# A fourth outer product split into seven inner products, in the first layer of two token chunks

## The chip, the cores and the metric

The kernel runs on one core of a Trainium2 chip. The metric is the device time of one execution in microseconds (us). Engines are called PE (TensorE), DVE (VectorE), ACT (ScalarE), POOL (GpSimd) and SP (the queue that issues most DMAs). Each engine takes its instructions strictly in the order in which they were issued.

## The reference

Attention with a hash mask over 4 x 8 heads of 768 tokens and 64 features, then a two-layer network on the 3072 x 512 result:

```python
scores = np.where(q_bucket == k_bucket, scale * q @ k.T, -1e9)
attn = softmax(scores) @ v               # (4, 8, 768, 64) -> x of (3072, 512)
h = x @ w_in                             # w_in  (512, 2048)
r = np.maximum(h, 0.0)
out = (r * r) @ w_out                    # w_out (2048, 512)
```

All of it is fp32.

## The kernel before

Attention comes first and fills the first 315 us. The network then takes the 3072 tokens in three chunks of 1024 (`i` = 0, 1, 2). For each chunk the first layer (`hidden` or `hidden_pair`) makes five sums of gated blocks, `b11, b12, b21, b22, b_t`, and the second layer (`project`) turns them into the output. The change is in the first layer of chunks 1 and 2.

**The outer scheme.** Each matrix product is done as 2 x 2 blocks with seven block products instead of eight (Strassen's scheme in Winograd's form). The first layer's blocks are halves of the features (256), of the hidden units (1024) and of the tokens (512). One row `r` of 128 hidden units (there are 8 in a half, `NR`) therefore has seven *outer products*, each of two matmuls of 128 x 128 by 512 columns. They are numbered by weight factor and go with a combination of x: 0 with "11", 1 with "21", 2 with "t4", 3 with "t1", 4 with "t2", 5 with "t3", 6 with "22". `w_unit` holds the weight factors of one row in the places that `PLACE` names. Chunk 0 does all seven so, in `hidden`.

**The inner scheme.** Chunks 1 and 2 go by *pairs* of rows (`hidden_pair(i, n, half)`, rows `n` and `n + 4`, four pairs in a chunk, half 0 and half 1). Products 1, 2 and 6 of both rows of a pair are done together, once more as 2 x 2 blocks (two rows, two feature blocks, two token quarters of 256): seven *inner products* of one 128 x 128 matmul by 256 columns in place of eight. `inner_steps` returns these seven in four steps, with the engines' work that belongs to them. In PSUM they use `acc1`, into which products 0, 4, 5 and 2 are added one after the other, with a copy on ScalarE taken between them (`one`, `two`, `three`); `acc2`; and `last`, a part of the tile `acc3`, whose two banks are the two sides. A is the set for product 1, C for product 2, B for product 6. `put(unit, out, other)` adds the outer part and gates one row: `gated` is relu(h) * h in a single VectorE operation (L921).

Products 0, 3, 4 and 5 of each row stay outer products (L1108) in `hidden_pair`; 0, 4 and 5 add up in `acc0`, again with a ScalarE copy between them (`keep`, L1116), and 3 goes into `acc2`. Matmuls of the inner sets are on L1061.

**Order.** The order of every engine is written out by hand (`tc.manual_schedule()`): an engine's instructions run as the Python code issues them, and the framework adds only semaphore waits for data and for reused buffers. Buffers named "h" (`new_h`, five of them, `NH`) hold the halves of a row until it is gated; a new one waits until an earlier holder has been read for the last time. `mark` is a Square over part of q or k on ScalarE (`peak`, L891), four in a pair, whose sums decide on a fallback that does not run here. Weights of the next pair come on SP's queue: `load_unit` (one row's `w_unit`, two buffers) and nine loads of `load_inner` and `load_third_inner`.

**The second layer.** `project(i)` runs seven outer products `k`, each as seven inner products of four matmuls of 256 columns (`product`, L844). In each, `hook` issues VectorE work after the second inner product has been issued, and ScalarE copies out (`one`, `two`, `five`, `three`) stand in ScalarE's queue in the order of issue. `sums_inner` makes the x sums that the inner sets read; for A, B and C it ran in the hooks of k = 5 and k = 6 of the layer before. `inner_sums(0, ...)` makes, a pair at a time, those that product k = 0 reads.

## Time and profile before

| | |
|---|---|
| median of 3 runs | 856.15 us (855.42 to 856.63) |
| the profiled execution | 855.04 us, its span 853.2 us |
| attention | up to 315.5 us in the span |
| network, chunk 0 (both layers) | 315.5 to 496.4 us |
| first layer, chunk 1 | 496.4 to 588.0 us |
| second layer, chunk 1 | 588.0 to 672.6 us |
| first layer, chunk 2 | 672.6 to 764.1 us |
| second layer, chunk 2 | from 764.1 us |

Times in profile lines are from the start of the span. In a row of groups, `x600 | 133.0, 379 | 0.0` reads: 600 instructions, 133.0 us busy in all, 379 ns each on average, 0.0 us idle just before them. In timeline rows the columns are start, duration, engine, line, operation, tiles written and read; a bracket at the end gives the engine's idle time before it and whom it waited for.

### The profile page before, as it was taken

To read this page: it belongs to the slowest core of one execution; us is meant where nothing else is said; L and a number is where in the kernel's file an instruction comes from. 1 tells how busy PE (TensorE), PEld (TensorE's weight loads), DVE (VectorE), ACT (ScalarE), POOL (GpSimd) and SP (SyncE) were. 2 spreads that over 40 slices of the span, in tenths; PEclk is the share of its full clock that TensorE was granted. 3 is DMA by queue.
4 is the path that set the end of the run, shared out by engine and by line. 5 is a ranking of instruction groups with operands and counts; after the bars stand their busy time and mean duration, and the time that the engine had idled before them with its cause. 6 is when DMAs were issued, how large, how long until landed. Compare 5 with 4: busy or idle time off the path is not lost.

```text
span 853.2 us, 17058 instructions
## 1 busy us (share of the span) xinstructions
PE 847.0 (99%) x6625; PEld 526.5 (62%) x6625; DVE 749.3 (88%) x1025; ACT 402.4 (47%) x752; POOL 167.4 (20%) x282
## 2 busy tenths in 40 slices
PE   8999999999999999999999999999999999999998
PEld 4544444444444444444788866667888765668886
DVE  5999999999999988988899968888988788889777
ACT  6877777888877752222211145554111355541111
POOL 2311111123221101543122121111000311200003
PEclk9999999999999999999999999999999999999999
DMA  9776988979998526999976985437647865335467
GB/s 213 137 152 143 183 181 203 209 158 258 242 227 217 170 69 225 342 313 297 340 250 220 275 214 189 160 111 283 192 155 189 205 219 171 128 118 161 140 172 147
DMA packets 232052, 170.12 MB, mean 199 GB/s; under 512 B 164712, under 2 KB 189104, under 8 KB 231968
## 3 DMA queue, kind: packets, MB, share of 16 engines
q1 hardware_dynamic: 192272, 87.78, 41.3%
q0 software_dynamic: 16512, 42.45, 15.9%
q10 hardware_dynamic: 23184, 38.78, 14.6%
q8 instruction: 53, 0.87, 0.4%
q14 instruction: 31, 0.25, 0.1%
HBM read 127.14 MB, written 41.16 MB: 197 GB/s over the span
## 4 chain that ended last, share of the span: by engine, by line
PE 97%; DVE 1%; DMA 1%; issue 0%; ACT 0%; SPq 0%; ACTq 0%; DVEq 0%
PE acc L844 39%; PE st L438 18%; PE xo L492 15%; PE acc L1108 13%; PE acc L1061 9%; PE tot L541 2%; PE hash L368 1%; DMA out_dram<-h 1%; DMA qk_nat<-in_q_dram 0%; PE tp L324 0%; DVE h L1224 0%; DVE o L1210 0%; DVE tmp L1210 0%; DVE bits L418 0%; DVE sum L1210 0%
## 5 line engine op out<-in xcount | busy, mean ns | idle before, releaser
L444 ACT ACTIVATE e<-st 128x768 f32<-128x768 f32 x192 | 155.4, 810 | 57.8 <-PE st L438 54.7
L438 PE MATMUL st<-feat 64*64 64x384 f32 x1536 | 156.9, 483 | 0.1
L492 PE MATMUL xo<-e,v_nat 64*64 64x385 f32 (+1 forms) x1520 | 156.7, 483 | 0.0
L844 PE MATMUL acc<-b,leaf 128*128 128x256 f32 x600 | 133.0, 379 | 0.0
L844 PEld LDWEIGHTS acc<-b,leaf 128*128 128x128 f32 x600 | 113.9, 190 | 16.0 <-issue 0.5
L480 DVE TENSOR_TENSOR total<-total,e 128x1536 f32<-128x1536 f32 x64 | 111.8, 1746 | 4.3 <-ACT e L444 2.8
L404 POOL DMA_DIRECT2D bits<-signed x120 | 61.9, 520 | 216.8 <-ACT signed L393 199.9
L492 PEld LDWEIGHTS xo<-e,v_nat 64*64 64x64 f32 (+1 forms) x1520 | 55.5, 133 | 68.2 <-issue 60.2
L1108 PE MATMUL acc<-t_x,w_unit 128*128 128x512 f32 x192 | 90.9, 595 | 0.0
L438 PEld LDWEIGHTS st<-feat 64*64 64x64 f32 x1536 | 55.4, 133 | 38.9 <-issue 34.9
L844 PE MATMUL acc<-t,leaf 128*128 128x256 f32 x336 | 76.0, 379 | 0.0
L844 PEld LDWEIGHTS acc<-t,leaf 128*128 128x128 f32 x336 | 63.8, 190 | 8.8 <-issue 0.2
L921 DVE SCALAR_TENSOR_TENSOR b<-h 128x512 f32<-128x512 f32 x96 | 65.7, 691 | 3.0
L438 PE MATMUL st<-bits 64*64 64x384 bf16 x768 | 64.7, 325 | 0.3 <-DVE bits L422 0.2
L844 PE MATMUL acc<-x,w_unit 128*128 128x512 f32 x128 | 56.5, 593 | 0.0
L851 ACT COPY two<-acc 128x256 f32<-128x256 f32 (+1 forms) x29 | 12.5, 431 | 87.5 <-PE acc L844 65.9
L844 PE MATMUL acc<-b_t,leaf 128*128 128x256 f32 x240 | 53.8, 379 | 0.0
L1108 PEld LDWEIGHTS acc<-t_x,w_unit 128*128 128x128 f32 x192 | 35.8, 190 | 26.7 <-issue 23.0
L1229 POOL DMA_DIRECT2D out_dram<-h x24 | 15.5, 655 | 181.9 <-DVE h L1224 181.9
L844 PEld LDWEIGHTS acc<-b_t,leaf 128*128 128x128 f32 x240 | 45.6, 190 | 6.2
L851 ACT COPY one<-acc 128x256 f32<-128x256 f32 (+1 forms) x29 | 12.5, 431 | 78.2 <-PE acc L844 58.8
L438 PEld LDWEIGHTS <-bits 64*64 64x64 bf16 x768 | 23.2, 107 | 38.0 <-issue 37.9
(180 smaller groups left out, 1289.0 us busy)
## 6 DMA issues: line engine op xcount, KB each, us to landing
leaf<-w_out ACTq DMA_DIRECT2D x142, 256.0 KB, 3.1
raw<-in_moe_w_in_dram SPq DMA_DIRECT2D x8, 1024.0 KB, 6.7
raw<-in_moe_w_out_dram SPq DMA_DIRECT2D x8, 1024.0 KB, 7.9
w_unit<-w_in SPq DMA_DIRECT2D x16, 512.0 KB, 4.1
w_unit<-w_in SPq DMA_DIRECT2D x8, 896.0 KB, 9.0
w_out<-sums POOLq DMA_DIRECT2D x16, 448.0 KB, 8.0
v_nat<-in_v_dram SPq DMA_DIRECT2D x16, 384.0 KB, 5.2
x_all<-x_t SPq DMA_DIRECT2D x16, 384.0 KB, 3.3
```

The source lines that it names most:

```text
L404: nc.gpsimd.dma_start(out=t[h * D:h * D + NBITS + 1, w, c * HS:(c + 1) * HS], in_=signed[at:at + NBITS + 1, h],)
L438: nc.tensor.matmul(out=st[k * HK:(k + 1) * HK, h, 0:HS], lhsT=src[1][rows, key], rhs=src[0][rows, cut], start=first, stop=not first, skip_ ...
L444: nc.scalar.activation(out=key_of(pr, kt)[:, :, i, 0:HS], in_=st[:, :, 0:HS], func=ACTF.Exp, scale=scale)
L480: nc.vector.tensor_tensor(out=totals[pr], in0=totals[pr], in1=e, op=ALU.add)
L492: return nc.tensor.matmul(out=outs[pr][h * D:(h + 1) * D, c, 0:HS + 1], lhsT=nat[pr, "v_nat"][rows, h, kt * D:(kt + 1) * D], rhs=key_of(pr ...
L541: done = nc.tensor.matmul(out=spares[pr][g * 32:(g + 1) * 32, c2, 0:QS], lhsT=ones[rows], rhs=totals[pr][rows, h, c, c2 * QS:(c2 + 1) * QS ...
L844: nc.tensor.matmul(out=acc[to], lhsT=a(i), rhs=b(i), start=first and i == 0, stop=last and i == n - 1, skip_group_check=True,)
L851: nc.scalar.copy(out=t, in_=acc[of])
L921: nc.vector.scalar_tensor_tensor(out=out, in0=h, scalar=0.0, in1=h, op0=ALU.max, op1=ALU.mult)
L1061: nc.tensor.matmul(out=out, lhsT=w(a), rhs=b, start=start, stop=stop, skip_group_check=True)
L1108: nc.tensor.matmul(out=to, lhsT=w[:, PLACE[a], f], rhs=bt[b](f), start=first and f == 0, stop=last and f == NFT // 2 - 1, skip_group_check ...
L1229: queue.dma_start(out=out[at, m0 + a * 32:m0 + (a + 1) * 32].rearrange("(c i) j -> i c j", i=32), in_=ot[a * 32:(a + 1) * 32].rearrange("i ...
```

## The change

Product 3 (with "t1") of both rows of a pair becomes a fourth inner set, D (`j` = 3). Its weight sums live in `w_unit` itself: `load_unit` loads one more block for the pair's first row, and `sum_unit` forms four sums of 128 columns on VectorE, one pair ahead (for a chunk's first pair, in the second layer before). Its x sums are made by `sums_inner(i, (3,))` in the first pair, where those of set 1 move too.

The sets now run two at a time: A and D step by step in half 0, C and B in half 1; before, A, B and C were spread with one or two between two outer products. `acc2` is no longer used by outer products. The steps `two` and `five` are copied straight into the "h" buffers (D's first unit takes the buffer `five`), and the additions that follow are put into `adds`.

The gate of b22 moves from VectorE (one operation) to ScalarE (`gate_b22`, Relu and then Square). Three parts at the end of a pair (`behind_pair`: the b21 units and two differences on VectorE, the gate of row n + 4 on ScalarE) are issued inside the next pair's half 0, and for the last pair in the hook of k = 0 of the second layer. The `tmp` tiles of the second layer become two halves of one tile.

```diff
@@ load_unit, and new functions beside it
+            if n >= NR and n % 2 == 0:
+                nc.sync.dma_start(out=w_unit[n][:, 4], in_=w_in_7[NQ + r, :, PLACE[3]])
+    def own_factors(w):
+        a = PLACE[3]
+        return (w[:, a, 0], w[:, a, 1], w[:, 4, 1]) + tuple(w[:, 5 + n // 2, n % 2] for n in range(4))
+    def sum_unit(n):
+        if n < NCHUNK * NR:
+            w = w_unit[n]
+            a11, a12, a22, *sums = own_factors(w)
+            sums_a(a11, a12, w[:, 4, 0], a22, *sums)
@@ inner_steps
+            side = j % 2
+            one = three = t_inner[i][3 * side][3]
+            last = snaps[i][:, side, 0:QN]
+            def new(unit):
+                if j == 3 and unit == 0:
+                    return p_r.tile([P, 512], FP32, name="five", bufs=KEPT["five"])
+                return new_h()
...
             def step_1():
-                hs["a2"] = last
-                mul(hs["a0"], 4, t[:, 1], False, False)
-                nc.scalar.copy(out=two, in_=hs["a0"])
-                mul(hs["a2"], 3, t[:, 0], True, False)
-                nc.scalar.copy(out=five, in_=hs["a2"])
+                mul(hs["a0"], 4, t[1], False, False)
+                nc.scalar.copy(out=hs[0][:, QN:HN], in_=hs["a0"])
+                mul(last, 3, t[0], True, False)
+                hs[1] = new(1)
+                nc.scalar.copy(out=hs[1][:, QN:HN], in_=last)
 
             def step_2():
                 mul(hs["a0"], 5, t3, False, False)
                 nc.scalar.copy(out=three, in_=hs["a0"])
-                mul(hs["a2"], 6, y22, False, True)
-                nc.vector.tensor_tensor(out=hs[0][:, QN:HN], in0=hs["a2"], in1=two, op=ALU.add)
-                hs[1] = new_h()
-                nc.vector.tensor_tensor(out=hs[1][:, QN:HN], in0=three, in1=five, op=ALU.add)
+                mul(last, 6, y22, False, True)
+
+            def adds():
+                for unit, by in (0, last), (1, three):
+                    h = hs[unit][:, QN:HN]
+                    nc.vector.tensor_tensor(out=h, in0=h, in1=by, op=ALU.add)
@@ hidden_pair, as it is after the change
+            def gate_b22(r, h):
+                nc.scalar.activation(out=h, in_=h, func=ACTF.Relu)
+                nc.scalar.activation(out=b22[:, r], in_=h, func=ACTF.Square)
...
+            add(0, "11", True, False)
+            one = keep("one")
             if half == 0:
                 A[0]()
+                D[0]()
+                if n == 0:
+                    sums_inner(i, (1,))
+                else:
+                    behind_pair[0]()
+            else:
+                B[0]()
+                C[0]()
+                gate_b22(r0, fives[0])
+                B[1]()
+                A[4](1, b11[:, r], one)
+                if n + 1 < NQ:
+                    sum_unit(i * NR + 2 * n + 2)
+            mark(0)
+            add(4, "t2", False, False)
+            two = keep("two")
+            if half == 0:
+                A[1]()
+                D[1]()
+                if n:
+                    behind_pair[1]()
             else:
                 B[2]()
+                C[1]()
+                B[3]()
+                C[2]()
+                B[5]()
                 B[4](0, b12[:, r0], now["two"])
+                C[5]()
+                add_in(two, fives[1])
+                B[4](1, b12[:, r], two)
                 minus(b_t[:, r0], b12[:, r0], b11[:, r0])
+                minus(b_t[:, r], b12[:, r], b11[:, r])
+                inner_sums(0, slice(n, n + 1))
+            mark(1)
+            add(5, "t3", False, True)
+            three = keep("three")
             if half == 0:
                 A[2]()
+                D[2]()
+                A[3]()
+                D[3]()
+                A[5]()
+                D[5]()
+                add_in(two, fives[0])
+                add_in(fives[0], three)
                 A[4](0, b11[:, r], one)
+                if n:
+                    behind_pair[2]()
             else:
                 C[3]()
+                three_0 = now["three"]
+                def sums():
+                    minus(b12[:, r0], b22[:, r0], b12[:, r0])
+                    add_in(fives[1], three)
+                    C[4](0, b21[:, r0], three_0)
+                    C[4](1, b21[:, r], three)
+                behind_pair[:] = (
+                    sums, lambda: gate_b22(r, fives[1]),
+                    lambda: minus(b12[:, r], b22[:, r], b12[:, r]),
+                )
@@ project
                     sum_x(i + 1, 2)
+                    sum_unit((i + 1) * NR)
...
                     y21 = b[:, NQ:NR, 0:QN]
                     minus(y21, y21, t2)
+                    if k == 0:
+                        for step in behind_pair:
+                            step()
+                        behind_pair.clear()
...
-                        sums_inner(i + 1, (0, 1))
+                        sums_inner(i + 1, (0,))
```

More of the change, by code (lines that the diff above doesn't have):

```diff
@@ L951, in hidden @@
             )
-        w_inner, t_inner, snaps, now = {}, {}, {}, {}
+        w_inner, t_inner, snaps, now, behind_pair = {}, {}, {}, {}, []
         thirds = {}
@@ L1028, in quarters_x @@
         def quarters_x(i, j):
-            x = xs[i][0]
-            b = (x[:, 2:4, 0:HN], x[:, 0:2, HN:NCH], x[:, 2:4, HN:NCH])[j]
+            x, t_x = xs[i]
+            b = (x[:, 2:4, 0:HN], x[:, 0:2, HN:NCH], x[:, 2:4, HN:NCH], t_x[0])[j]
             return b[:, 0, 0:QN], b[:, 0, QN:HN], b[:, 1, 0:QN], b[:, 1, QN:HN]
@@ L1036, in sums_inner, with inner_steps @@
             for j in js:
-                t = p_y.tile([P, NQ, QN], FP32, name=f"t{j}", **({"bufs": 2} if j < 2 else {}))
+                if j < 3:
+                    tile = p_y.tile([P, NQ, QN], FP32, name=f"t{j}", **({"bufs": 2} if j < 2 else {}))
+                    t = [tile[:, m] for m in range(NQ)]
+                else:
+                    os = [p_y.tile([P, HN], FP32, name="o", bufs=NOUT) for _ in range(2)]
+                    t = [o[:, m * QN:(m + 1) * QN] for o in os for m in range(2)]
                 t_inner.setdefault(i, {})[j] = t
                 y11, y12, y21, y22 = quarters_x(i, j)
-                minus(t[:, 0], y12, y11)
-                minus(t[:, 1], y22, t[:, 0])
-                minus(t[:, 2], y21, t[:, 1])
+                minus(t[0], y12, y11)
+                minus(t[1], y22, t[0])
+                minus(t[2], y21, t[1])
                 minus(y12, y22, y12)
-        def inner_steps(i, n, j):
-            w, t = w_inner[i, n][j], t_inner[i][j]
+        def inner_steps(i, n, j, w):
+            t = t_inner[i][j]
             y11, t3, y21, y22 = quarters_x(i, j)
-            hs = {}
-            if i not in snaps:
-                o = [p_y.tile([P, HN], FP32, name="o", bufs=NOUT) for _ in range(2)]
-                o = [o[m // 2][:, m % 2 * QN:(m % 2 + 1) * QN] for m in range(3)]
-                snaps[i] = o, [t_inner[i][m][:, 3] for m in range(3)], spare("acc3")
-            side = (3 * n + (0, 2, 1)[j]) % 2
-            one, two, five = snaps[i][side]
-            three = one
-            last = snaps[i][2][:, side, 0:QN]
+            if i not in snaps:
+                snaps[i] = spare("acc3")
+            side = j % 2
+            one = three = t_inner[i][3 * side][3]
+            last = snaps[i][:, side, 0:QN]
+            hs = {}
+            def new(unit):
+                if j == 3 and unit == 0:
+                    return p_r.tile([P, 512], FP32, name="five", bufs=KEPT["five"])
+                return new_h()
             def mul(out, a, b, start, stop):
@@ L1069, in step_0 @@
                 mul(a1, 1, y21, True, True)
-                hs[0] = new_h()
+                hs[0] = new(0)
                 nc.vector.tensor_tensor(out=hs[0][:, 0:QN], in0=a1, in1=one, op=ALU.add)
@@ L1083, in step_2 @@
                 nc.scalar.copy(out=three, in_=hs["a0"])
-                mul(hs["a2"], 6, y22, False, True)
-                nc.vector.tensor_tensor(out=hs[0][:, QN:HN], in0=hs["a2"], in1=two, op=ALU.add)
-                hs[1] = new_h()
-                nc.vector.tensor_tensor(out=hs[1][:, QN:HN], in0=three, in1=five, op=ALU.add)
+                mul(last, 6, y22, False, True)
[3 more added lines that the diff above has]
+                    nc.vector.tensor_tensor(out=h, in0=h, in1=by, op=ALU.add)
             def step_3():
-                mul(hs["a0"], 2, t[:, 2], False, True)
+                mul(hs["a0"], 2, t[2], False, True)
                 nc.scalar.copy(out=hs[1][:, 0:QN], in_=hs["a0"])
@@ L1096, in put @@
                 gated(out, h)
-            return step_0, step_1, step_2, step_3, put
+            return step_0, step_1, step_2, step_3, put, adds, hs
         def hidden_pair(i, n, half):
@@ L1104, in hidden_pair, with add @@
             acc = ps_m.tile([P, 512], FP32, name="acc0")
-            def add(to, a, b, first, last):
+            def add(a, b, first, last):
                 for f in range(NFT // 2):
                     nc.tensor.matmul(
-                        out=to, lhsT=w[:, PLACE[a], f], rhs=bt[b](f),
+                        out=acc, lhsT=w[:, PLACE[a], f], rhs=bt[b](f),
                         start=first and f == 0, stop=last and f == NFT // 2 - 1,
@@ L1112, in add, with keep @@
                     )
-            def keep(of, name):
-                t = p_r.tile([P, 512], FP32, name=name, bufs=KEPT[name])
-                nc.scalar.copy(out=t, in_=of)
+            def keep(name):
+                if (name, half) == ("two", 0):
+                    t = p_y.tile([P, HN], FP32, name="tmp")
+                else:
+                    t = p_r.tile([P, 512], FP32, name=name, bufs=KEPT[name])
+                nc.scalar.copy(out=t, in_=acc)
                 return t
@@ L1120, in mark, with add_in @@
                 peak(2 * ((i - 1) * NR + 2 * n + half) + m)
+            def add_in(out, by):
+                nc.vector.tensor_tensor(out=out, in0=out, in1=by, op=ALU.add)
+            def gate_b22(r, h):
+                nc.scalar.activation(out=h, in_=h, func=ACTF.Relu)
+                nc.scalar.activation(out=b22[:, r], in_=h, func=ACTF.Square)
             if half == 0:
@@ L1124, in hidden_pair @@
                 load_third_inner(i, n + 1, nc.sync)
-                now["A"], now["C"], now["B"] = (inner_steps(i, n, j) for j in range(3))
-            A, B, C = (now[c] for c in "ABC")
-            add(acc, 0, "11", True, False)
-            one = keep(acc, "one")
+                if n == 0:
+                    sums_inner(i, (3,))
+                own = own_factors(w)
+                now["A"] = inner_steps(i, n, 0, w_inner[i, n][0])
+                now["D"] = inner_steps(i, n, 3, lambda a: own[a])
+            else:
+                C, B = (inner_steps(i, n, j, w_inner[i, n][j]) for j in (1, 2))
@@ L1129, in hidden_pair @@
+            A, D = now["A"], now["D"]
+            fives = D[6]
+            add(0, "11", True, False)
+            one = keep("one")
             if half == 0:
                 A[0]()
+                D[0]()
+                if n == 0:
+                    sums_inner(i, (1,))
+                else:
+                    behind_pair[0]()
+            else:
+                B[0]()
[5 more added lines that the diff above has]
+                    sum_unit(i * NR + 2 * n + 2)
@@ L1131, in hidden_pair @@
+            mark(0)
[6 more added lines that the diff above has]
+                    behind_pair[1]()
             else:
                 B[2]()
-                C[0]()
-                A[4](1, b11[:, r], one)
+                C[1]()
+                B[3]()
+                C[2]()
+                B[5]()
                 B[4](0, b12[:, r0], now["two"])
-            mark(0)
@@ L1137, in hidden_pair @@
-            other = ps_m.tile([P, 512], FP32, name="acc2")
-            add(other, 3, "t1", True, True)
-            five = keep(other, "five")
-            if half == 0:
-                A[1]()
-            else:
-                B[3]()
-                C[1]()
-                minus(b_t[:, r0], b12[:, r0], b11[:, r0])
-                minus(b12[:, r0], b22[:, r0], b12[:, r0])
-            add(acc, 4, "t2", False, False)
-            two = keep(acc, "two")
+                C[5]()
+                add_in(two, fives[1])
@@ L1149, in hidden_pair @@
+                B[4](1, b12[:, r], two)
+                minus(b_t[:, r0], b12[:, r0], b11[:, r0])
+                minus(b_t[:, r], b12[:, r], b11[:, r])
[3 more added lines that the diff above has]
+            three = keep("three")
             if half == 0:
                 A[2]()
-                B[0]()
-                A[4](0, b11[:, r], one)
-                nc.vector.tensor_tensor(out=two, in0=two, in1=five, op=ALU.add)
-            else:
-                C[2]()
-                nc.vector.tensor_tensor(out=two, in0=two, in1=five, op=ALU.add)
-                B[4](1, b12[:, r], two)
-                minus(b_t[:, r], b12[:, r], b11[:, r])
-                inner_sums(0, slice(n, n + 1))
-                C[4](0, b21[:, r0], now["three"])
@@ L1161, in hidden_pair @@
-            mark(1)
-            add(acc, 5, "t3", False, True)
-            three = keep(acc, "three")
-            if half == 0:
-                A[3]()
-                B[1]()
-                gate_sum(b22[:, r], three, five)
+                D[2]()
[5 more added lines that the diff above has]
+                add_in(fives[0], three)
+                A[4](0, b11[:, r], one)
+                if n:
+                    behind_pair[2]()
@@ L1168, in hidden_pair @@
             else:
                 C[3]()
-                gate_sum(b22[:, r], three, five)
-                minus(b12[:, r], b22[:, r], b12[:, r])
-                C[4](1, b21[:, r], three)
+                three_0 = now["three"]
[8 more added lines that the diff above has]
+                )
@@ L1210, in add_to @@
             nc.vector.tensor_tensor(out=out, in0=one, in1=two, op=ALU.add)
+        turns = []
         def whole(one, two):
@@ L1215, in whole @@
                 return one
-            t = p_y.tile([P, QN], FP32, name="tmp", bufs=2)
-            add_to(t, one, two)
-            return t
+            turns.reverse()
+            add_to(turns[0], one, two)
+            return turns[0]
         def put_out(i, ih, jh, n, o):
@@ L1272, in project @@
             V, W, U, X = (p_y.tile([P, 4, QN], FP32, name=f"sum{n}") for n in range(4))
+            tmp = p_y.tile([P, HN], FP32, name="tmp")
+            turns[:] = tmp[:, 0:QN], tmp[:, QN:HN]
             outs = {}
```

## The prediction

> **What bounds the kernel now.** I read the head of the page first, then the chain of work that ended last, and then the same chain in order of time.

> ```profile
> span 853.2 us, 17058 instructions
> PE 847.0 (99%) x6625; PEld 526.5 (62%) x6625; DVE 749.3 (88%) x1025; ACT 402.4 (47%) x752; POOL 167.4 (20%) x282
> PEclk9999999999999999999999999999999999999999
> PE 97%; DVE 1%; DMA 1%; issue 0%; ACT 0%; SPq 0%; ACTq 0%; DVEq 0%
> ```

> TensorE (PE) is busy 99% of the span at full clock and is 97% of the chain. In the stage that the change edits, the chain in order of time (start, us, engine, line, records; an fp32 product is two records) shows one pair, and then the start of the second layer:

> ```profile
> 519.33 1.72 PE acc L1108 x4
> 521.05 0.86 PE acc L1061 x4
> 521.91 1.72 PE acc L1108 x4
> ...
> 526.21 1.73 PE acc L1061 x8
> ...
> 539.98 1.79 PE acc L1108 x4
> 542.21 1.72 PE acc L1108 x4
> ...
> 587.96 84.61 PE acc L844 x392
> ```

> An outer product (L1108, two 512-column matmuls) takes 1.72 us, one 256-column inner product (L1061) 1.73/4 = 0.432, and a pair 542.21 - 519.33 = 22.88. By count that is 8 x 1.72 + 21 x 0.432 = 22.83, so TensorE stands still for 0.05 us in a pair. Whatever the change saves in products it gets in full, if it adds no wait; every wait that it adds is paid in full.

> How close the others are is seen in the busy times of that pair (columns: window, sum, PE, PEld, DVE, ACT, POOL, each with its instructions, clock, DMA share, GB/s):

> ```profile
> 519.30:542.20 22.90, 22.90 (x76) 14.00 (x75) 18.98 (x35) 12.84 (x32) 4.29 (x9) 1.00 0.51 175
> ```

> VectorE (DVE) is busy 83% and ScalarE (ACT) 56%, so both have room on average. What decides is order: all engines take their instructions in turn.

> **What TensorE gains.** Each pair loses two outer products (the t1 product of each half) and gets seven inner products: 2 x 1.72 - 7 x 0.432 = 0.42 us. If the present 0.05 us of waiting goes too, it is 0.46 us, and over the 8 pairs (4 in each of two chunks) **-3.7 us**. A pair would then take 6 x 1.72 + 28 x 0.432 = 22.42 us.

> The other engines' work in a pair, counted in the code: VectorE has 22 operations of 512 columns and 12 of 256, and will have 20, 15 and 4 of 128; ScalarE has 8 copies of 512, 15 of 256 and 4 peak steps, and will have 6, 20, 4 and two gates of two passes. By the times below ScalarE goes from 11.7 us to 14.5 in 22.4: more, and still not full.

> **The durations for the walk.** The timeline around the end of chunk 2's pairs gives start-to-start times (start, us, engine):

> ```profile
> 584.71 1.03 PE L1061 MATMUL acc<-x,sum 128*128 128x256 f32 x4
> 584.91 0.58 ACT L1116 COPY two<-acc 128x512 f32<-128x512 f32 x1 [1.34 <-PE acc L1108]
> 585.39 0.38 ACT L1083 COPY t<-acc 128x256 f32<-128x256 f32 x1
> 585.57 1.96 PE L1108 MATMUL acc<-t_x,w_unit 128*128 128x512 f32 x4
> 585.66 0.86 ACT L891 ACTIVATE raw_qk<-raw_qk 128x768 f32<-128x768 f32 x1
> 586.12 0.42 DVE L1087 TENSOR_TENSOR h<-t,t 128x256 f32<-128x256 f32 x1
> 586.40 0.20 ACT L891 ACTIVATION_READ_ACCUMULATOR raw_qk<-raw_qk 128x1 f32 x1
> 586.45 0.69 DVE L1156 TENSOR_TENSOR two<-two,five 128x512 f32<-128x512 f32 x1
> 587.17 0.69 DVE L1095 TENSOR_TENSOR h<-h,two 128x512 f32<-128x512 f32 x1
> 587.37 0.59 PE L1061 MATMUL acc<-t,sum 128*128 128x256 f32 x2
> 587.57 0.59 ACT L1116 COPY three<-acc 128x512 f32<-128x512 f32 x1 [0.97 <-PE acc L1108]
> 587.89 0.69 DVE L921 SCALAR_TENSOR_TENSOR b<-h 128x512 f32<-128x512 f32 x1
> 588.62 0.69 DVE L600 TENSOR_TENSOR b_t<-b,b 128x512 f32<-128x512 f32 x1
> 589.23 0.42 DVE L600 TENSOR_TENSOR t<-b 128x256 f32<-128x256 f32 x1
> 589.68 0.42 DVE L600 TENSOR_TENSOR t<-b,t 128x256 f32<-128x256 f32 x1
> 590.02 0.42 DVE L600 TENSOR_TENSOR b<-b 128x256 f32<-128x256 f32 x1
> ...
> 595.07 1.22 DVE L600 TENSOR_TENSOR b<-b,t 128x1024 f32<-128x1024 f32 x1
> 596.20 1.22 DVE L600 TENSOR_TENSOR t<-b 128x1024 f32<-128x1024 f32 x1
> ```

> VectorE: 512 columns 0.72 to the next if that reads its result (586.45 to 587.17), 0.60 if not (588.62 to 589.23); 256 columns 0.45 and 0.34; 1024 columns 1.13. ScalarE: a 512-column copy 0.48, a 256-column copy 0.27, the peak step 0.94 (585.66 to 586.40, and 0.20). Hand-overs: a product's result is copied 0.20 after TensorE goes on (587.37, 587.57). TensorE follows a copy's end by 0.16: `two` ends at 585.49, and the matmul behind it (1.96, not 1.88) got going 0.08 after 585.57. VectorE to ScalarE takes 0.10:

> ```profile
> 523.05 0.68 DVE L930 TENSOR_TENSOR h<-three,five 128x512 f32<-128x512 f32 x1
> ...
> 523.83 0.58 ACT L1116 COPY five<-acc 128x512 f32<-128x512 f32 x1 [1.05 <-DVE h L930]
> ```

> The new Relu and Square of 512 columns in SBUF are not in the trace. The nearest rows are the 0.58 of the copy above, and a 512-column Relu with a bias tile:

> ```profile
> L166 ACT ACTIVATE small<-power,excess 128x512 uint8<-128x512 uint32 x32 | 23.0, 717 | 0.7 <-DVE power L150 0.7
> ```

> I take 0.65 between 0.58 and 0.72: Relu 0.70 until Square, which reads it (0.05 more, as on VectorE), and Square 0.55 to the next, which overlaps it by 0.10, as copies do. [...]

> **Three new waits**, walked from the start of a pair (0) with nothing late: outer product 1 to 1.72, A[0] and D[0] to 3.45, product t2 to 5.17, A[1] 6.03, D[1] 6.89, product t3 8.61, A[2] and D[2] 10.34, then A[3]; the second half starts at 11.20.

> *Wait 1, D[1], every pair.* Step 1's second product writes acc3 (`last`). A and D now run it one right behind the other, on two halves of one tile, and the built program makes D's wait for the ScalarE copy of A's. A's ends at 6.03, its copy runs from 6.23 to 6.61, TensorE goes on at 6.77 and not at 6.46: 0.31, x 8 = **2.5 us**. Before, a 1.72 us outer product lay between such steps.

> *Wait 2, A[3], pairs 2 to 4 of a chunk.* All five "h" buffers are held when a pair ends: D's second unit, B's two and C's two. In the next pair A takes B's, and D's second unit the one of C's first unit, which is free only when `behind_pair[0]` has gated that into b21. So the ScalarE copy in D[1] waits for VectorE, whose queue runs without a gap from B[5] of the pair before; B[5] starts when C[2]'s last product is readable, at 20.25 + 0.20 of that pair, that is -1.97. Then: B[5] and C[5] 4 x 0.34; B[4](0) 0.72 + 0.60; add_in 0.72; B[4](1) 0.72 + 0.60; two b_t 1.20; inner_sums 0.45 + 0.34 + 0.34; A[0], D[0] 0.68; minus and add_in 1.20; C[4](0) 0.72 + 0.73 to its end: 10.4, so 8.4. ScalarE copies at 8.5 (to 8.8), Relu to 9.5, Square to 10.0, the peak step to 11.0, `three` to 11.45; A[2]'s copy ends at 11.85, and A[3], which adds into the bank just copied, goes at 12.0. TensorE was there at 10.34 + 0.31. **1.35 us** x 6 = **8.1 us**. Queued behind that one copy are thus both gate steps, the peak step, `three` and A[2]'s copy; TensorE waits for the last of them.

> *Wait 3, the first product of the second layer.* The rest of the last pair is issued in the hook of k = 0. VectorE, from -1.97 again: 7.05 to the end of inner_sums (5.1); the hook's 1024-column minus 1.13 (6.2); minus 0.60; add_in 0.69 (7.5). ScalarE's Relu starts at 7.6, Square at 8.3, and the copy of `two`, queued behind both, at 8.9; it ends at 9.25, TensorE goes on at 9.4. Four groups of four products, 4 x 1.73, had it there at 6.9: **2.5 us** x 2 = **5.0 us**. Then nothing is late: k = 1 starts at some 14.6, and what it reads first leaves VectorE by 10.8 (C[4] twice 1.32, minus 0.60, after 7.5).

> **Costs taken at nothing.** The added weight load (128 KB, 4 times a chunk, on SP's queue in front of nine loads for the next pair) and sum_unit's four 128-column operations, at most 4 x 0.42, which wait for it:

> ```profile
> w_unit<-w_in SPq DMA_DIRECT2D x16, 512.0 KB, 4.1
> sum<-w_in SPq DMA_DIRECT2D x16, 128.0 KB, 4.1
> ```

> They are issued as D[3] ends, and VectorE comes to them some 5 us later, 4.1 needed. It next waits for C[2], some 3 us after; that is the cover, and beyond it each microsecond of late landing moves wait 2 by one. The eight sums of `sums_inner` moved or added in pair 1 (3.2 us) stand where no `behind_pair` is queued.

> **Sum.** 855.04 us is the profiled execution's time, 1.8 above its span; -3.7 + 2.5 + 8.1 + 5.0 = +11.9 gives 866.9. The median of the runs is 1.1 higher (856.15), so **868.0 us**. Bounds: gate 0.58 to 0.72, twice in 8 stalls, -1.1 to +1.1; wait 1 absent -2.5, and with it a pair's A[3] is reached sooner, which wait 2 gives back; each VectorE walk 0.3 short or 0.5 long, x 8, -2.4 to +4.

> [...] L921 gates 512 columns in one VectorE operation of 0.69 us; ScalarE needs two of about 0.65. [...] With the gate on VectorE, 1.25 us leave ScalarE's queue in waits 2 and 3, so that 0.1 of each wait 2 and nothing of wait 3 would be left: 12.5 us less, 855.5, if VectorE has room for two more gates in a pair.

> **Rivals.**
> *The count alone (faster).* ScalarE is idle 44% of a pair; if the copy in D[1] finds its buffer free before 6.9 (decides: VectorE's backlog at a pair's start under 6.8 us and not 10.4), waits 2 and 3 vanish and so, if acc3's halves are independent, does wait 1: 856.15 - 3.7 = 852.5. For: the room above. Against: the queue of single steps is fixed. 3%.
> *Wait 2 half hidden.* VectorE keeps ahead because TensorE's own waits give it time: two of the six remain, 868.0 - 5.4 = 862.6. Against: B[5] starts anew from TensorE in each pair. 12%.
> *Late weights (slower still).* sum_unit's loads land over 8 us after issue, as with the page's 9.0 for 896 KB; in-order VectorE then starts B[5] 2 us late, 6 x 2 = 12: 880. Decides at 8 us. 8%.
> *The change does nothing* (products saved equal waits added, within the 0.2%, 1.7 us, that runs of this kernel can tell from no change): 856. 2%.

> **Numbers.** The forecast has 75%, with 864 to 872 as its own range. 861.5 to 874.5 takes in the half-hidden case and leaves out count alone, nothing and late weights. Faster 0.03, same 0.02, slower 0.95.

> **What would show it.** In the changed profile: a pair of about 24.1 us in the chain (22.7 for a chunk's first), the second layer's first product 2.5 us longer; waits listed as PE behind ScalarE copies (`last` 0.3 us x 8, `three` 1.3 x 6, `two` of the second layer 2.4 x 2), and ScalarE's copy into h behind VectorE's gate into b21. Pairs of 22.4 us would prove the count alone; ScalarE or VectorE waiting for a load of w_unit, late weights.

## The result and the profile after

The change makes the kernel slower: a median of 869.61 us (six runs, 867.61 to 871.01) against 856.44 us of the kernel before on the same chip (855.42 to 857.02), a ratio of 1.0154 (95% interval 1.0141 to 1.0167). 868.0 us had been forecast, within 861.5 to 874.5. The profiled execution took 867.61 us, 12.57 more than before.

The head of the page after the change, the busy times and the shares of the chain:

```profile
span 866.1 us, 17328 instructions
...
PE 849.2 (98%) x6673; PEld 535.4 (62%) x6673; DVE 753.3 (87%) x1073; ACT 425.1 (49%) x808; POOL 167.4 (19%) x282
...
PE 86%; DVE 9%; ACT 2%; issue 1%; POOL 0%; ACTq 0%; DVEq 0%; POOLq 0%
```

Before, TensorE was 97% of the chain; now VectorE (9%) and ScalarE (2%) hold pieces of it: TensorE waits for them in turn.

To compare kernels apart from the start and the end of the program I use the *network stretch*, from the network's first product to the last matmul. Its two ends in the timeline of before:

```profile
315.43 1.98 PE L844 MATMUL acc<-x,w_unit 128*128 128x512 f32 x4
...
849.32 0.44 PE L1260 MATMUL acc<-ident,o 128*128 128x128 f32 x2 [0.52 <-DVE o L1210]
```

and of after:

```profile
316.41 1.98 PE L858 MATMUL acc<-x,w_unit 128*128 128x512 f32 x4
...
861.05 0.44 PE L1324 MATMUL acc<-ident,o 128*128 128x128 f32 x2 [0.52 <-DVE o L1272]
```

533.89 us became 544.64, +10.75. The other 2.1 us of the longer span lie where the code is the same: 0.98 ahead of 316.41, 1.1 behind the last matmul. These two ends differ by more between profiles of one and the same code there: 315.43 and 3.9 in the kernel before, 317.92 and 5.1 in e7 below.

Two pairs of chunk 1 in the view by windows (the first pair, then the second):

```profile
497.36:520.08 22.72, 22.69 (x81) 15.12 (x81) 14.53 (x35) 14.12 (x35) 4.13 (x8) 1.00 0.67 185
520.08:543.90 23.82, 22.92 (x81) 15.04 (x80) 19.10 (x40) 15.60 (x39) 4.25 (x9) 1.00 0.53 173
```

A pair took 22.88 before. The first of a chunk is shorter now, as forecast (22.7), the others longer (23.82; forecast 24.1). Where the second pair loses time is seen in its timeline (rows of PE and ScalarE):

```profile
526.10 1.32 PE L1082 MATMUL acc<-o,w_unit 128*128 128x256 f32 x4
...
528.56 0.37 ACT L1100 COPY h<-acc 128x256 f32<-128x256 f32 x1 [1.45 <-DVE b L935]
528.83 0.64 ACT L1153 ACTIVATE h<-h 128x512 f32<-128x512 f32 x1
...
529.49 0.63 ACT L1154 ACTIVATE b<-h 128x512 f32<-128x512 f32 x1
...
530.03 0.83 ACT L905 ACTIVATE raw_qk<-raw_qk 128x768 f32<-128x768 f32 x1
...
530.85 0.56 ACT L1142 COPY three<-acc 128x512 f32<-128x512 f32 x1
...
531.32 0.37 ACT L1104 COPY t<-acc 128x256 f32<-128x256 f32 x1
...
531.74 0.70 PE L1082 MATMUL acc<-t,sum 128*128 128x256 f32 x2 [0.87 <-ACT t L1104]
```

The first row is wait 1: four records (two products) that take 1.03 without a wait take 1.32. The others are wait 2 with the whole queue: D[1]'s copy waits 1.45 for VectorE's gate into b21, then Relu, Square, peak step, `three` and A[2]'s copy follow without a gap, and A[3] is the last row. Wait 3, in the second layer's first product:

```profile
599.33 0.69 DVE L1118 TENSOR_TENSOR h<-h,three 128x512 f32<-128x512 f32 x1
599.45 0.63 ACT L1153 ACTIVATE h<-h 128x512 f32<-128x512 f32 x1 [5.26 <-DVE h L1149]
...
600.11 0.63 ACT L1154 ACTIVATE b<-h 128x512 f32<-128x512 f32 x1
...
600.65 0.35 ACT L865 COPY two<-acc 128x256 f32<-128x256 f32 x1
...
601.05 1.13 PE L858 MATMUL acc<-b,leaf 128*128 128x256 f32 x4 [1.83 <-ACT two L865]
```

ScalarE stood idle for 5.26 us in front of the Relu, because that comes first in its queue, ahead of the copy of `two` that TensorE waits for.

### The profile page after: what moved, and what is told of

It reads as the page before. It is cut to its first block, busy times and chain, and to the rows that moved or that the text cites. A ratio compares the mean times of both kernels' runs of the same rounds, so it can differ in the third digit from the quotient of the medians.

```text
span 866.1 us, 17328 instructions
## 1 busy us (share of the span) xinstructions
PE 849.2 (98%) x6673; PEld 535.4 (62%) x6673; DVE 753.3 (87%) x1073; ACT 425.1 (49%) x808; POOL 167.4 (19%) x282
## 3 DMA queue, kind: packets, MB, share of 16 engines
q10 hardware_dynamic: 23184, 38.78, 14.5%
## 4 chain that ended last, share of the span: by engine, by line
PE 86%; DVE 9%; ACT 2%; issue 1%; POOL 0%; ACTq 0%; DVEq 0%; POOLq 0%
PE acc L858 39%; PE st L438 18%; PE xo L492 14%; PE acc L1082 7%; PE acc L1131 4%; DVE h L1118 2%; DVE b L935 2%; PE tot L541 2%; DVE h L1110 1%; PE hash L368 1%; DVE b L600 1%; DVE b_t L600 1%; ACT raw_qk L905 1%; DVE two L1149 1%; DVE h L1149 1%
## 5 line engine op out<-in xcount | busy, mean ns | idle before, releaser
L1131 PE MATMUL acc<-t_x,w_unit 128*128 128x512 f32 x128 | 60.1, 592 | 0.0
L935 DVE SCALAR_TENSOR_TENSOR b<-h 128x512 f32<-128x512 f32 x80 | 54.6, 691 | 2.5
L865 ACT COPY two<-acc 128x256 f32<-128x256 f32 (+1 forms) x29 | 12.5, 430 | 81.5 <-PE acc L858 69.1
L865 ACT COPY one<-acc 128x256 f32<-128x256 f32 (+1 forms) x29 | 12.5, 431 | 78.2 <-PE acc L858 63.6
L1110 DVE TENSOR_TENSOR h<-h,acc 128x256 f32<-128x256 f32 x24 | 10.1, 419 | 41.6 <-PE acc L1082 34.5
## 6 DMA issues: line engine op xcount, KB each, us to landing
w_unit<-w_in SPq DMA_DIRECT2D x16, 512.0 KB, 4.1
```

The costliest lines, as they stand in the source:

```text
L865: nc.scalar.copy(out=t, in_=acc[of])
L935: nc.vector.scalar_tensor_tensor(out=out, in0=h, scalar=0.0, in1=h, op0=ALU.max, op1=ALU.mult)
L1110: nc.vector.tensor_tensor(out=h, in0=h, in1=by, op=ALU.add)
L1131: nc.tensor.matmul(out=acc, lhsT=w[:, PLACE[a], f], rhs=bt[b](f), start=first and f == 0, stop=last and f == NFT // 2 - 1, skip_group_chec ...
```

## The experiments

All runs are set against the kernel before on the same chip. "Pair" is the second pair of chunk 1; "half clock" counts the stretches at half TensorE clock (PEclk 0.50) in the profiled network stretch (told below).

| kernel | median us | ratio to before (95%) | network stretch | pair | half clock |
|---|---|---|---|---|---|
| before | 856.44 | | 533.89 | 22.88 | 0 |
| after | 869.61 | 1.0154 (1.0141 to 1.0167) | 544.64 | 23.82 | 0 |
| e1 | 864.98 | 1.0089 (1.0072 to 1.0106) | 543.09 | 22.69 | 2 |
| e2 | 862.79 | 1.0070 (1.0053 to 1.0086) | 539.59 | 22.68 | 1 |
| e3 | 869.45 | 1.0141 (1.0116 to 1.0166) | 545.84 | 23.82 | 0 |
| e4 | 867.54 | 1.0119 (1.0102 to 1.0136) | 543.83 | 23.82 | 0 |
| e5 | 862.50 | 1.0072 (1.0055 to 1.0089) | 540.00 | 22.73 | 1 |
| e6 | 862.98 | 1.0072 (1.0056 to 1.0089) | 540.96 | 23.83 | 0 |
| e7 | 888.64 | 1.0371 (1.0354 to 1.0389) | 567.25 | 27.07 | 7 |
| e8 | 859.54 | 1.0034 (1.0024 to 1.0043) | 537.34 | 22.43 | 1 |
| e9 | 853.11 | 0.9963 (0.9951 to 0.9976) | 530.94 | 22.39 | 0 |
| e10 | 854.60 | 0.9983 (0.9972 to 0.9994) | 530.86 | 22.39 | 0 |

### e1: the gates back on VectorE

```diff
             def gate_b22(r, h):
-                nc.scalar.activation(out=h, in_=h, func=ACTF.Relu)
-                nc.scalar.activation(out=b22[:, r], in_=h, func=ACTF.Square)
+                gated(b22[:, r], h)
```

> The changed kernel with both gates of b22 in a pair done by one VectorE operation each, instead of Relu and Square on ScalarE. Prediction's theory (ScalarE's queue holds the gate in front of what TensorE waits for): wait 2 falls from 1.1-1.3 us to about 0.1 and wait 3 from 2.3 to nothing, 12.5 us less than predicted for the change, that is some 10.5 us less than the 869.6 measured: 857 to 859. Rival (VectorE's backlog): wait 2 goes, but the gates' 0.7 us stand in VectorE's queue, which is already late at the end of a chunk's pairs; the 2.3 us of wait 3 leave the copy of `two` and come back one product later, in k = 1 of the second layer, where TensorE waits for VectorE: 863 to 864.

864.98 us, 4.6 less than after the change and 6 to 8 short of the theory. Wait 2 is gone (pair 22.69), but in k = 1 TensorE waits 2.34 and 2.44 us in the two chunks, and each of these waits was followed by a stretch at half clock (PEclk 0.50 from 616 to 618 and from 796 to 798). The rival holds, 1 us above its range. Unforeseen by both, a chunk's first pair grew from 22.68 to 23.24; why stays open.

### e2: the deferred gate behind D[2]

```diff
                 D[1]()
-                if n:
-                    behind_pair[1]()
...
                 D[2]()
+                if n:
+                    behind_pair[1]()
                 A[3]()
```

> The changed kernel with one line moved: in the first half of pairs 2 to 4 the deferred ScalarE gate is issued behind D[2] instead of behind D[1]; the five h buffers and the copy in D[1] that waits for one of them stay. Theory (the gate's 1.3 us stand behind that copy and in front of `three` and A[2]'s copy): A[3]'s wait of 1.1 us in 6 pairs falls to 0.1 or less, 6 to 7 us less: 862.5 to 863.5; wait 1 (0.3 us, 8 times) and wait 3 (2.3 us, twice) stay. Rival (the held h buffer itself is what TensorE waits for, whatever stands behind the copy): no change, 869.6.

862.79 us, as the theory has it. Timeline, PE and ScalarE, at the place shown above:

```profile
527.79 0.37 ACT L1100 COPY h<-acc 128x256 f32<-128x256 f32 x1 [1.45 <-DVE b L935]
528.06 0.85 ACT L905 ACTIVATE raw_qk<-raw_qk 128x768 f32<-128x768 f32 x1
...
529.37 0.38 ACT L1104 COPY t<-acc 128x256 f32<-128x256 f32 x1
...
529.95 0.59 PE L1082 MATMUL acc<-t,sum 128*128 128x256 f32 x2
530.04 0.63 ACT L1153 ACTIVATE h<-h 128x512 f32<-128x512 f32 x1
```

The copy still waits 1.45 for its buffer and the gate is still on ScalarE; only the place of 1.3 us in the queue has changed, and TensorE's wait in front of A[3] is gone.

### e3: the last gate of a chunk on VectorE

```diff
-                    sums, lambda: gate_b22(r, fives[1]),
+                    sums, lambda: gate_b22(r, fives[1]) if n + 1 < NQ else gated(b22[:, r], fives[1]),
```

> The changed kernel with the gate that is issued in the second layer's first product (once a chunk) on VectorE; all other gates stay on ScalarE. Prediction's theory (Relu and Square stand in front of the copy of `two`): the 2.3 us of wait 3 go, twice: 865.0. Rival (VectorE's backlog at the end of the pairs is the cause, ScalarE only where it shows): the copy of `two` is on time, but the next product's fifth group waits 2.5 us for VectorE's difference, so 869.6 to 870.0.

869.45 us: no gain. The wait at `two` has gone; in its place (timeline of k = 1, VectorE and PE):

```profile
608.57 4.49 DVE L600 TENSOR_TENSOR b<-b,b_t 128x2048 f32<-128x2048 f32 x2
...
612.98 1.22 DVE L600 TENSOR_TENSOR t<-b_t 128x1024 f32<-128x1024 f32 x1
...
614.23 1.23 DVE L600 TENSOR_TENSOR t<-b_t,t 128x1024 f32<-128x1024 f32 x1
615.37 1.22 DVE L600 TENSOR_TENSOR b_t<-b_t 128x1024 f32<-128x1024 f32 x1
616.51 1.22 DVE L600 TENSOR_TENSOR b<-b,t 128x1024 f32<-128x1024 f32 x1
...
617.83 1.53 PE L858 MATMUL acc<-b,leaf 128*128 128x256 f32 x6 [2.34 <-issue]
```

TensorE's wait is put down to "issue", that is to nothing that the profile shows, but VectorE works without a gap up to it. The difference at 616.51 is what the product at 617.83 reads; in front of it stand five operations, 7.9 us, that only k = 2 and k = 5 need. In the changed kernel, wait 3 itself gave VectorE the time to catch up: there the same difference ended at 616.28, and TensorE came to its product at 616.70.

### e4: A's `last` product first

```diff
             def step_1():
-                mul(hs["a0"], 4, t[1], False, False)
-                nc.scalar.copy(out=hs[0][:, QN:HN], in_=hs["a0"])
+                def four():
+                    mul(hs["a0"], 4, t[1], False, False)
+                    nc.scalar.copy(out=hs[0][:, QN:HN], in_=hs["a0"])
+                if j:
+                    four()
                 mul(last, 3, t[0], True, False)
                 hs[1] = new(1)
                 nc.scalar.copy(out=hs[1][:, QN:HN], in_=last)
+                if not j:
+                    four()
```

> The changed kernel with A's two products of step 1 exchanged, so that 0.86 us lie between A's product into acc3 and D's. Theory: the 0.3 us that D's product waits for ScalarE's copy of A's go in all 8 pairs; 6 of the pairs give it back, since TensorE is then 0.3 us earlier at A[3], where it waits for ScalarE: 2 x 0.3 = 0.6 us less, 869.0, with wait 2 at 1.4 us and not 1.1. Rival (the two halves of acc3 hold each other up in any order): the wait of 0.3 us stays 8 times, 869.6.

The stretch is 0.81 us shorter (0.6 expected) and the second pair still 23.82, for the reason given: waits of TensorE, after the change (engine, tile, line, whom it waited for: us in total, times, longest)

```profile
PE acc L1082 <- ACT t L1104: 5.2, 6, 0.9
```

and with e4:

```profile
PE acc L1082 <- ACT t L1110: 7.0, 6, 1.2
```

Wait 1 is gone, and wait 2 takes it back: (7.0 - 5.2)/6 = 0.3 us each. The median fell by more, 2.1 us; what of that is clock is told below.

### e5: D's second unit straight in b22

```diff
                     return p_r.tile([P, 512], FP32, name="five", bufs=KEPT["five"])
+                if j == 3:
+                    return b22[:, NQ + n]
                 return new_h()
```

> The changed kernel with D's second unit put straight into the rows of b22 that its gate fills (Relu and Square then work in place there), so that it needs no h buffer; the gate stays where it is in ScalarE's queue. Theory (the copy in D[1] waits because the fifth h buffer is held until VectorE has gated C[4](0)): that copy no longer waits, everything queued behind it moves up, and A[3] waits under 0.3 us instead of 1.1: 5 to 6.5 us less than 869.6, 863.1 to 864.6. Rival (b22 is followed as one tile, and the copy now waits for the gate and the difference that use other rows of it, or the gate alone fills ScalarE's time): A[3] waits as before, 869.6.

862.50 us, a little better than expected. e2 moved the gate and kept the buffer; this keeps the gate's place and takes the buffer away. Both remove wait 2, so it took both: a copy held up by a buffer, and a queue behind that copy.

### e6: e3, and sums for later products issued later

```diff
                     minus(y21, y21, t2)
+                    if k == 1 and i:
+                        for h in range(2):
+                            at_h = slice(h * NQ, (h + 1) * NQ)
+                            minus(b11[:, at_h], b22[:, at_h], b_t[:, at_h])
+                        inner_sums(2)
...
-                if k == 0:
+                if k == 0 and i == 0:
```

The first part is in `hook`; the last line keeps the old place, behind the product k = 0, for chunk 0 alone.

> The kernel with the last gate on VectorE (e3), and, in the last two chunks, the two 2048-column differences into b11 and the sums for k = 2 issued after the first difference of k = 1 instead of before it. Theory (wait 3 is VectorE's backlog: its 2.3 us come back in k = 1 because VectorE works off 5.6 us of sums for later products first): no wait over 0.3 us in k = 0 or k = 1, 2 x 2.3 = 4.6 us less than e3's 869.5: 864.9, and up to 1.7 us less again if a stall of that length also costs clock. Rival (the backlog is still there one product on, or the ScalarE copy `two` has another cause): the wait moves to k = 2, 869.5.

862.98 us, 6.5 under e3, and 4.9 in the stretch. Where e3's chain broke off ahead of 617.83, it now runs through the second layer's beginning in one piece of TensorE, up to 622, where this view of the chain ends:

```profile
592.62 29.40 PE acc L858 x135
```

So two waits of about one size stand in a row. The first, behind ScalarE's gate in front of `two`, hid the second, VectorE's lateness in k = 1; e3 took away the first, and the moved sums the second. The moved sums with the last gate left on ScalarE were not run. In the changed kernel VectorE comes to these sums at 607.12, long after the addition that the Relu waits for (its end is 599.41), so nothing here says that moving them would shorten wait 3 itself.

### e7: the kernel before with its gates on ScalarE

```diff
             h = new_h()
             nc.vector.tensor_tensor(out=h, in0=one, in1=two, op=ALU.add)
-            gated(out, h)
+            nc.scalar.activation(out=h, in_=h, func=ACTF.Relu)
+            nc.scalar.activation(out=out, in_=h, func=ACTF.Square)
```

(only for the two calls that fill b22)

> The kernel before, with no other edit than the two gates of b22 in a pair done by Relu and Square on ScalarE. Theory (place in the queue, not room on the engine): the second gate waits for VectorE's late sum at the end of a pair and stands in front of the copy `one` and A[0]'s copy of the next pair, so TensorE waits 2.4 us at A[1] in 6 pairs and 2.9 us in the second layer's first product twice: 20 us more than the kernel before, 876 to 877. Rival (ScalarE is idle 44% of a pair and hides two gates of 1.3 us): no change, 856.4. [...]

888.64 us: 32 more than before, 12 more than the theory. The waits are where they were expected, and about as long:

```profile
PE acc L1067 <- ACT t L1074: 8.9, 4, 2.2
PE acc L844 <- ACT one L851: 5.3, 2, 2.7
PE acc L1067 <- ACT o L1074: 4.5, 2, 2.2
```

Eight waits, 18.7 us of idle time. Most of the rest is clock: seven of the eight are followed by a stretch at half clock, 7 x 1.7 = 11.9. The one pair whose wait was not took 25.38 us and not 27.07. Of the 33.4 us by which the stretch grew, 2.8 are left, some 0.3 a wait; wait 2 too costs its pair 0.3 more (23.82 - 22.68 = 1.14) than its idle time says (0.87).

### e8: e4 and e5 together

> The changed kernel with two edits at once: D's second unit in b22 (e5) and A's two products of step 1 exchanged (e4). Theory (wait 1 is a true 0.3 us in each pair, given back in six pairs only as long as wait 2 stands behind it): with wait 2 gone the full 8 x 0.3 = 2.4 us come on top of e5: 861 to 862, where e4 alone brought 0.8 us in the profiled stretch. Rival (they are one wait): the same as e5, 863 to 864.5.

859.54 us, 3.0 under e5 and 1.5 under the range expected, and a pair of 22.43, 0.30 under e5's: x 8 it is the 2.4 of the theory. With wait 2 gone, wait 1 counts in full.

### e9 and e10: all cures

e9 joins e2, e4, e5 and e6 (whose last gate is on VectorE). e10 has e4, e5 and the moved sums of e6, and all gates on VectorE.

> The changed kernel with the cures of all three waits together: D's second unit in b22 (e5), A's two products of step 1 exchanged (e4), the deferred gate issued behind D[2] (e2), the last gate of a chunk on VectorE and the sums for later products behind k = 1's first difference (e6). The other gates stay on ScalarE. Theory (waits 1 to 3 and the clock that the long ones cost are the whole of what the change lost): a pair of 22.4 us, no wait over 0.3 us in the two chunks, full clock, so the 3.7 us of saved products less some 1 us of small waits are left: 2.7 us under the kernel before, 853 to 854. Rival (a further cost of the change, such as the added weight load or VectorE's share, shows once these are gone): 856 or more.

> As the run with all cures, but every gate of b22 on VectorE and none on ScalarE (so nothing is moved behind D[2]). Theory (what counts is what stands behind a gate in its queue; once VectorE's sums for later products are moved and D needs no h buffer, either engine hides it): the same 853 to 854. Rival (VectorE, at over 85% of a pair, is too full for two more gates of 0.7 us, as with e1): waits of 2 us at the start of the second layer again, 858 or more.

853.11 us, as expected, and 854.60, 0.6 above: both beat the kernel before, by 0.37% and 0.17%. In the stretch they don't differ (530.94 and 530.86); whether their medians do, these runs don't settle. The second pair of e9 by windows:

```profile
518.89:541.28 22.39, 22.39 (x81) 15.19 (x80) 18.92 (x40) 15.61 (x39) 4.26 (x9) 1.00 0.57 184
```

TensorE is busy all the time, with ScalarE as full (15.61) as after the change (15.60): room was never short. Of the 3.9 us that the pairs gain, e9's stretch keeps 2.95: the chunks' last pairs took 22.77 and 22.47, and the second layer's fifth group starts 7.18 us after the layer's first product, where it was 6.91, in both chunks. With the three waits and the one behind wait 3 cured, no larger cost of the change is left. e10 shows, against its rival, that VectorE too has room for the gates, once its order is right.

## Why the prediction was right, step by step

It came out right in size and in mechanism: three waits, each where it was expected. What it had wrong is the time with the gates on VectorE, since it did not see the wait that stands behind wait 3.

**The gain** was -3.7 by count. e9's pair gives 8 x (22.39 - 22.88) = -3.9. The rival of the count alone, 852.5, took all the cures to come near: e9 has 853.11.

**Wait 1**: 2.5 forecast. 22.68 (first pair, by its first products' starts) - 22.39 = 0.29, x 8 = 2.3.

**Wait 2**: 8.1 forecast, 6 x (23.82 - 22.68) = 6.8 measured. The chain was right link by link: the copy came 8.48 us after the pair's start (8.5 forecast), Relu and Square took 0.66 and 0.54 to the next instruction (0.70 and 0.55 taken; each is 0.63 to 0.64 long, 0.65 taken). The term mis-sized is the rest of that queue: the peak step took 0.82 to `three` (0.94 taken), and A[3] went 0.42 behind the start of A[2]'s copy (0.55 taken), so it went at 11.66 and not at 12.0. All six of these waits are alike, 0.87 to 0.88 us of idle time, so the rival by which VectorE catches up in four of them did not come.

**Wait 3**: 5.0 forecast, 4.6 measured: the fifth group of four products started 9.16 and 9.26 us after its layer's first product in the two chunks, and 6.91 in the kernel before, so 2.25 and 2.35 late. The steps held as well: in chunk 1 the Relu started 7.56 us after the layer's first product (7.6 forecast), Square at 8.22 (8.3), the copy of `two` at 8.76 (8.9), and TensorE went on at 9.16 (9.4). What the walk has no term for is the second wait of that size behind it: "what it reads first leaves VectorE by 10.8" leaves out the sums for k = 2 and k = 5, 7.9 us in VectorE's queue, in front of what k = 1 reads last (e3, e6). For the forecast this cost nothing, since wait 3 covers it.

**Costs taken at nothing.** No wait for a load of `w_unit` shows, so the late weights didn't come. Not priced was a queue at a chunk's last pair, where the first loads for the second layer are issued on ScalarE (timeline after the change, rows of ScalarE and PE):

```profile
580.55 2.52 ACTq L1262 DMA_DIRECT2D leaf<-w_out  x5
...
583.12 0.59 ACT L1142 COPY one<-acc 128x512 f32<-128x512 f32 x1 [2.20 <-PE acc L1082]
583.60 0.38 ACT L1089 COPY t<-acc 128x256 f32<-128x256 f32 x1
583.86 0.39 ACT L1089 COPY o<-acc 128x256 f32<-128x256 f32 x1
...
584.03 1.13 PE L1082 MATMUL acc<-t,leaf 128*128 128x256 f32 x4
```

Five issues hold ScalarE for 2.52 us, up to 583.07, and the copies come late (the profile puts the first one's wait down to TensorE, which had gone on from that product at 582.07); the last pairs are 24.17 and 24.01 long and not 23.82, 0.5 us in all. e9 still has it. Sum: -3.9 + 2.3 + 6.8 + 4.6 + 0.5 = +10.3 of the 10.75. The forecast's +11.9 for the stretch was 1.2 too high, and 2.1 us at the program's two ends, which no step of the change explains, made up for it: that is luck.

**The median** was forecast 1.1 above the profiled time; it lies 2.0 above. Five of the six runs have a mean clock of 0.996 to 0.997, the profiled one 0.998, and the profile shows half clock only from 863.10 on, behind the last matmul; a half-clock stretch that costs 1.7 us is 0.002 of the span. In e8, whose profiled run (0.996) has one such stretch, the four runs with 0.996 to 0.997 average 860.42 and the six with 0.998 to 0.999 average 858.66, 1.8 less. The four runs of e4, whose wait 3 is the same, have 0.998 to 1.000, and their median fell by 2.1 where the stretch fell by 0.8. That such a stretch makes the difference here is likely and not shown: only the profiled runs left a trace.

**The gates on VectorE.** 855.5 by the prediction's working, if VectorE has room; e1 took 864.98. The step that failed is "nothing of wait 3 would be left": what is left is the wait behind it, 2.34 and 2.44 us in k = 1 with a half-clock stretch each. In the kernel before, with its queue as it stands, VectorE was the better place: e7, with the gates on ScalarE, lost 32 us. It isn't a matter of the engine as such: e9 keeps seven of eight gates a chunk on ScalarE and is as short in the stretch as e10 with none there.

## What to carry to other kernels

Where engines work off their queues in order, as here (ScalarE idle for 5.26 us in front of wait 3's Relu, with the copy of `two` behind it), price what stands *behind* an added instruction, not the engine's idle share: ScalarE was idle about a third of a pair after the change, and moving one 1.3 us gate by two steps was worth 7 us. Before a wait is put down to the instruction in front of it, ask whether the engine that feeds it is late anyway: then curing the place alone moves the wait to a later product, and work that isn't needed yet has to be moved too. A saving in products is then banked by cures of order, without any faster operation.

## What was not expected of the hardware

In some of these runs a wait of TensorE cost more than its length. e5, in the second layer's first product of chunk 2, the timeline of PE:

```profile
775.80 6.49 PE L858 MATMUL acc<-b,leaf 128*128 128x256 f32 x21 [1.93 <-ACT two L865]
```

and by windows (PEclk is the third figure from the end):

```profile
774.00:776.00 2.00, 0.20 (x1) 0.21 (x2) 1.97 (x4) 1.75 (x4) 0.00 (x0) 1.00 0.05 10
776.00:778.00 2.00, 2.00 (x6) 1.60 (x6) 1.97 (x4) 0.14 (x1) 0.00 (x0) 0.58 0.85 286
778.00:780.00 2.00, 2.00 (x7) 1.57 (x6) 1.97 (x3) 0.37 (x1) 0.00 (x0) 0.56 0.28 97
780.00:782.00 2.00, 2.00 (x11) 1.77 (x10) 1.97 (x5) 0.00 (x0) 0.00 (x0) 1.00 0.86 257
```

In these profiles it goes with where the wait falls. e7's seven stretches last 3.41 us each (by the mean clocks of windows of 2 us; 0.84, 0.50 and 0.81 from 528 to 534 for the first) and begin at 529.34, 556.65, 583.95, 611.26, 747.79, 775.10 and 802.41, at distances of 8, 8, 8, 40, 8 and 8 times 3.413 us: they lie on a grid of that step. In e1, e2, e5 and e8 two stretches each begin 53, 24, 24 and 24 such steps apart (in e5 at 776.33 and 858.24, the second one behind the last matmul). The grid of each other profile is had, with the same step, from one of its own half-clock stretches, behind the last matmul where there is none before. In e5 the wait that was followed lies whole in the step from 772.92 to 776.33, in which TensorE is busy for 1.48 us, and half clock begins where the step ends. The twelve waits that were followed left TensorE standing for 1.93 to 2.44 us of one step; of the ten others nine left at most 1.89, the wait being shorter or cut in two by the grid (e3's 2.44 us into 1.08 and 1.36), and one, in e7, 1.94.

What sets the step, and why the clock falls, no trace here shows.
